# Top-k attention and a routed MLP on one core: GpSimd's difference for the first fold waits for VectorE's minimum of the second fold

## The chip, the core and the metric

The kernel runs on one core of a Trainium2 chip. The engines named here are TensorE (PE in the profile, its weight loads PEld), VectorE (DVE), ScalarE (ACT), GpSimd (POOL) and SyncE (SP), which issues most transfers. Each engine works through its own queue of instructions in order; semaphores make one wait for another. The metric is device time in microseconds (us), from the first instruction to the end of the program. An instruction's row in the profile carries the line of the kernel that issued it (L351 is line 351).

## The reference

The input is attention over 8 batches with 8 heads, 576 tokens and a head size of 64, in which each query keeps only its 32 largest scores, and then a routed MLP with 8 experts: each of the 4608 tokens goes through the one expert with the largest gate.

```python
scores = scale * np.matmul(q, k.transpose(0, 1, 3, 2))
kth = np.partition(scores, -top_k, axis=-1)[..., -top_k:-top_k + 1]
scores = np.where(scores >= kth, scores, -1000000000.0)
attn = np.exp(scores - scores.max(-1, keepdims=True))
attn = attn / (attn.sum(-1, keepdims=True) + 1e-09)
x = (attn @ v).transpose(0, 2, 1, 3).reshape(4608, 512)
...
expert_idx = np.argmax(x @ w_gate, axis=1)
gate_w = softmax(x @ w_gate)[np.arange(4608), expert_idx]
for e in range(8):
    h = np.maximum(x[expert_idx == e] @ w1[e], 0.0)
    y[expert_idx == e] = h @ w2[e]
return gate_w[:, None] * y
```

## The kernel before

**Units and slots.** Two heads of one batch form a unit; there are 32 units. One slot handles two tiles of 128 queries each, with 576 scores for every query. Two units together have 9 slots (8 with two full tiles, one with the tails of 64 queries), so there are 144 slots. They follow each other in `loop()`, in an order that is written out by hand for TensorE, ScalarE and VectorE; GpSimd's instructions keep the order of the program where `in_turn` is put around them. Once the first batch has its tokens sorted into rows of `x_rows`, pieces of the routed MLP are put between the attention's matmuls.

**What a slot does for its scores.** TensorE multiplies queries by keys into PSUM (`products`, L314), three to four slots ahead. ScalarE copies the scores to SBUF (`scores`, L321, the tile `s`), in slot i for slot i + 3. VectorE then folds them (`folds`, `fold`, `fold_on`) and searches the 32nd largest score of each query (`search`). In the first 27 slots ScalarE computes the weights without a mask (`unmasked`, L497), marks the scores under the threshold (`shortfalls`, L470, which waits for the threshold `low`), and TensorE subtracts the marks while it transposes the weights (L516, L517). In the other slots GpSimd takes part in the mask (`less`, L489).

**The folds.** A row of 576 scores is folded in half: `h` holds the 288 larger ones of each pair, `l` the smaller ones. Then `h` is folded again into `few` (144 larger ones) and `hl` (144 smaller ones). `search` looks for maxima in `few` with MAX8 (L415), strikes the found ones out with MATCH_REPLACE8 (L434), and repeats this for four rounds of eight. After the first round the function `lists` adds the eight largest of `l` and twice of `hl` to `few` (L390).

**Which engine makes `l`.** In the first 27 slots the smaller ones aren't all made by VectorE. For most of these slots GpSimd makes `l` in two steps on the scores' bit patterns taken as 32-bit integers: the sum of both halves (`added`, L338), and later the sum minus the larger one (`folds`, L351), which leaves the smaller one. Both steps keep GpSimd's order. Five of the 26 folds of this kind, those whose slot puts the output rows together on GpSimd (`rows`, L655), have their `l` made by VectorE instead (L355). The first slot of all uses `fold`.

**The order around the change.** In slot i, VectorE first makes the folds of slot i + 1 (L346 `h`, L347 `few`, L349 `hl`), then searches slot i, and ends with the threshold `low` (L449). GpSimd's difference for slot i + 1 is put right behind the folds. Behind it in GpSimd's queue come: the sum for slot i + 2 where there is one (L338), which has to wait until `lists` of slot i has read the buffer that it writes (there are two `l` buffers); two small differences (`doubts`, L457 and L460); the bias for the weights (`nbias`, L428); where due, the logits (L641 to L646), the output rows (L655), and indirect transfers of rows (L723). The first MAX8 of the search for slot i + 1, one slot later, waits for that slot's difference, as does `lists`, which reads `l`. There is one buffer for `h`, so that the next `h` waits until the difference has read it.

**Numbers of buffers.** `s` has four buffers, `few` three, `hl` and `l` two, `h` one. SP's queue loads queries, keys and values of the units, the experts' weights and the sorted rows.

Of the kernel before, what the change touches and what calls it, by code (L numbers as in the profile page):

```python
# [13 lines left out]
ALU = mybir.AluOpType  # L14
# [3 lines left out]
WAIT = mybir.DependencyInfo(mybir.DependencyClass.Sync, mybir.DependencyReason.DATA)  # L18
# [27 lines left out]
def kernel(  # L46
# [47 lines left out]
    nc = tc.nc  # L94
# [10 lines left out]
    HF = S // 2  # L105
    QF = S // 4
# [160 lines left out]
    def in_turn(put):  # L267

        if not k.exact:
            tc.keep_in_program_order(put)  # L270
        return put
# [69 lines left out]
    def folds(s, l=None):  # L341

        f = SimpleNamespace(aside=l is not None)
        f.h = k.att.tile([P, 2, HF], F32, name="h", bufs=1)
        f.few = k.att.tile([P, 2, LW], F32, name="few", bufs=3)
        nc.vector.tensor_tensor(f.h, s[:, :, 0, :], s[:, :, 1, :], op=ALU.max)  # L346
        nc.vector.tensor_tensor(f.few[:, :, 0:QF], f.h[:, :, 0:QF], f.h[:, :, QF:HF], op=ALU.max)  # L347
        f.hl = k.att.tile([P, 2, QF], F32, name="hl", bufs=2)
        nc.vector.tensor_tensor(f.hl, f.h[:, :, 0:QF], f.h[:, :, QF:HF], op=ALU.min)  # L349
        if f.aside:  # L350
            f.made = in_turn(nc.gpsimd.tensor_tensor(l, l, f.h[:, :, :].bitcast(I32), op=ALU.subtract)).ins  # L351
            f.l = l[:, :, :].bitcast(F32)
        else:
            f.l = k.att.tile([P, 2, HF], F32, name="l")
            nc.vector.tensor_tensor(f.l, s[:, :, 0, :], s[:, :, 1, :], op=ALU.min)  # L355
        return f
# [791 lines left out]
    with fast:  # L1148
# [224 lines left out]
        def loop():  # L1373
# [16 lines left out]
            for i, (b, g) in enumerate(work):  # L1390
# [11 lines left out]
                if i + 1 < len(work):  # L1402
                    if quick(i):
                        def behind():
                            f_of[i + 1] = folds(s_of[i + 1], l_of.pop(i + 1, None))
                    else:
                        def behind():
                            f_of[i + 1] = fold(s_of[i + 1])

                        then = lambda: fold_on(f_of[i + 1], soon and not k.heavy)  # L1410
                    if i:
                        behind()
                        behind = lambda: None
# [227 lines left out]
```

## Time and profile before

| what | us |
|---|---|
| median of 3 runs | 1280.93 (1280.36 to 1282.18) |
| the profiled execution, its own time | 1280.47 |
| its span, first to last instruction | 1278.9 |
| TensorE busy in the span | 1197.5 (94%) |
| VectorE busy | 1058.1 (83%) |
| ScalarE busy | 922.3 (72%) |
| GpSimd busy | 721.3 (56%) |

The shares are means over stages of different kinds: the folds that the change concerns start between 18.2 and 208.1 us, the attention's slots go on until about 1070 us, and behind that only the routed MLP is left. So the profile is read by stages below, with the table of stretches, the waits between engines, the timeline of single slots, and the rows grouped by line. The mean granted TensorE clock of the execution was 0.97 of full speed.

### The profile page before, as it was taken

Reading aid. Unit: us, or ns where it says so; the run is one execution under the profiler, and the core shown is the slowest. Engines: PE = TensorE matmul, PEld = TensorE weight load, DVE = VectorE, ACT = ScalarE, POOL = GpSimd, SP = SyncE. Lnnn points to the kernel's source line nnn. Section 1 sums busy time; section 2 is a strip of 40 time slices with the busy share of each in tenths; the row PEclk is TensorE's granted clock in tenths of the full one; section 3 lists DMA queues with packets and bytes.
Section 4 is the critical chain, followed back from the end, with each engine's and each line's share of the span. In section 5 each row is a group of like instructions: output and inputs, shape, how many; then the busy total and the mean of one; then the engine's idle time right before and its main releaser. Section 6 shows DMA issues by size and latency. Waiting matters only on the chain. (4 is left out here: it accounts for less than half of the span.)

```text
span 1278.9 us, 26013 instructions
## 1 busy us (share of the span) xinstructions
PE 1197.5 (94%) x8312; PEld 852.9 (67%) x8312; DVE 1058.1 (83%) x4635; ACT 922.3 (72%) x2063; POOL 721.3 (56%) x1006
## 2 busy tenths in 40 slices
PE   6877778799899999999999999999999999999998
PEld 3555555566556665766667667676666667799985
DVE  8999999999999999999999999999999985000000
ACT  4677767898889888988888889888888892111211
POOL 4554454777787786657666775667656762100010
PEclk9788888899999999999999999999999999999999
DMA  5010011653174318542865464456554646995662
GB/s 154 27 34 23 12 31 56 239 189 103 61 268 166 114 55 308 204 137 95 284 229 191 162 234 179 179 187 215 186 195 167 231 162 221 360 352 210 237 238 83
DMA packets 97043, 216.58 MB, mean 169 GB/s; under 512 B 5245, under 2 KB 26237, under 8 KB 96896
## 3 DMA queue, kind: packets, MB, share of 16 engines
q1 hardware_dynamic: 89728, 194.54, 43.6%
q0 software_dynamic: 6352, 19.97, 4.3%
q8 instruction: 67, 1.10, 0.3%
q14 instruction: 80, 0.66, 0.2%
q10 hardware_dynamic: 816, 0.31, 0.1%
HBM read 191.42 MB, written 23.91 MB: 168 GB/s over the span
## 5 line engine op out<-in xcount | busy, mean ns | idle before, releaser
L489 POOL TENSOR_TENSOR w<-s,w 128x576 f32<-128x576 f32 x234 | 331.8, 1439 | 233.8 <-ACT w L480 233.7
L1102 PE MATMUL ph<-xTs,w 128*128 128x128 f32 x1984 | 249.6, 278 | 2.8 <-ACT xTs L993 2.8
L1102 PEld LDWEIGHTS ph<-xTs,w 128*128 128x128 f32 x1984 | 233.7, 192 | 26.8 <-issue 23.1
L1119 PE MATMUL py<-w,hT 128*128 128x512 f32 x496 | 239.0, 603 | 0.5
L415 DVE MAX8 tops<-few 128x8 f32<-128x144 f32 (+3 forms) x864 | 222.5, 292 | 0.0
L314 PE MATMUL sc<-qkb 64*128 64x288 f32 (+1 forms) x1280 | 204.8, 461 | 15.5 <-ACT s L321 11.3
L506 ACT ACTIVATE w<-w,nbias 128x576 f32<-128x576 f32 x234 | 181.2, 785 | 0.9 <-POOL w L489 0.3
L321 ACT COPY s<-sc 128x576 f32<-128x576 f32 x288 | 168.1, 635 | 8.3 <-PE sc L314 8.2
L480 ACT ACTIVATE w<-s,low 128x576 f32<-128x576 f32 x234 | 168.7, 768 | 3.8
L314 PEld LDWEIGHTS sc<-qkb 64*128 64x128 f32 (+1 forms) x1280 | 111.0, 190 | 83.8 <-issue 39.8
L434 DVE MATCH_REPLACE8 few<-tops,few 128x144 f32<-128x144 f32 (+2 forms) x576 | 158.1, 279 | 0.0
L521 ACT COPY wT<-wTm 128x512 f32<-128x512 f32 x234 | 127.2, 594 | 41.2 <-PE wTm L514 40.1
L514 PE MATMUL wTm<-turn,w 128*128 128x128 f32 x936 | 127.7, 277 | 21.6 <-ACT oT L591 11.0
L514 PEld LDWEIGHTS wTm<-turn,w 128*128 128x128 f32 x936 | 108.0, 143 | 56.6 <-issue 22.4
L586 PE MATMUL po<-wT,vb 128*64 128x288 f32 x1024 | 139.5, 415 | 0.0
L1119 PEld LDWEIGHTS py<-w,hT 128*128 128x128 f32 x496 | 84.2, 190 | 74.5 <-issue 72.5
L390 DVE MAX8 few<-l 128x8 f32<-128x288 f32 x288 | 127.0, 441 | 0.0
L1011 POOL DMA_INDIRECT out_dram<-y,xg x36 | 38.4, 1066 | 150.0 <-ACT y L1078 85.4
L586 PEld LDWEIGHTS po<-wT,vb 128*64 128x64 f32 x1024 | 68.3, 138 | 64.8 <-issue 12.5
L390 DVE MAX8 few<-hl 128x8 f32<-128x72 f32 x576 | 99.4, 211 | 0.0
L330 DVE TENSOR_TENSOR h<-s 128x576 f32<-128x576 f32 (+1 forms) x119 | 90.1, 757 | 2.8 <-ACT s L321 2.8
L434 DVE MATCH_REPLACE8 scr<-tops,few 128x168 f32<-128x168 f32 x288 | 88.5, 311 | 0.0
(234 smaller groups left out, 1969.5 us busy)
## 6 DMA issues: line engine op xcount, KB each, us to landing
w<-in_moe_w_dram SPq DMA_DIRECT2D x72, 2048.0 KB, 9.0
qkb<-in_qk_dram SPq DMA_DIRECT2D x31, 608.0 KB, 4.0
vb<-in_v_dram SPq DMA_DIRECT2D x32, 320.0 KB, 3.2
xg<-x_rows SPq DMA_DIRECT2D x36, 257.0 KB, 9.1
x_rows<-blank SPq DMA_DIRECT2D x13, 257.0 KB, 7.4
x_rows<-blank POOLq DMA_DIRECT2D x4, 257.0 KB, 9.3
x_rows<-x,posi POOLq DMA_INDIRECT x40, 3.4
out_dram<-y,xg POOLq DMA_INDIRECT x36, 4.0
```

What stands on the lines that cost most here:

```text
L314: nc.tensor.matmul(ps[rows, j, 0:HF], n.q[d, cols], n.k[d, keys], start=True, stop=True)
L321: lambda m=m, ps=ps: nc.scalar.copy(s[:, m, :, :], ps[:, :, 0:HF]) for m, ps in enumerate(got)
L390: nc.vector.max(out=f.few[:, m, QF + 8 * j:QF + 8 * j + 8], in_=away)
L415: scan = nc.vector.max(out=tops[:, m, r * 8:(r + 1) * 8], in_=src[m]).ins
L434: nc.vector.match_replace(out=src[m] if inside else scr[:, m, :], in_to_replace=tops[:, m, r * 8:(r + 1) * 8], in_values=src[m], imm_value ...
L480: nc.scalar.activation(w[:, m, :], s[:, m, :, :].rearrange("p j k -> p (j k)"), AF.Relu, scale=-STEEP, bias=low[:, m:m + 1],)
L489: k.last_pool = in_turn(nc.gpsimd.tensor_tensor(w[:, m, :], s[:, m, :, :].rearrange("p j k -> p (j k)"), w[:, m, :], op=ALU.subtract)).ins
L506: nc.scalar.activation(w[:, m, :], w[:, m, :], AF.Exp, scale=scale, bias=nbias[:, m:m + 1], accum_out=n.z[:, c:c + 1])
L514: nc.tensor.transpose(to, part(w), ident)
L586: nc.tensor.matmul(po[r, 0:HF], n.v[:, c, r], rhs, start=(c == 0), stop=(c == KC - 1))
L1102: nc.tensor.matmul(ph[:, f, :], n.w1[:, 0, dt, fc * P:(fc + 1) * P], n.xT[:, dt, :], start=(dt == 0), stop=(dt == DT - 1),)
L1119: nc.tensor.matmul(py, hT[:, f, :], n.w2[:, 0, f, :], start=(f == 0), stop=(f == FT - 1))
```

## The change

The difference on GpSimd (L351) is given a further dependency: it must wait until VectorE has finished the minimum of the second fold, `hl`. Before, it waited for `h`, which it reads, and for its own earlier sum. No instruction is added or taken away, and the order of each engine's instructions in the program is the same. The other branch, in which VectorE makes `l`, is as it was.

```diff
         f.hl = k.att.tile([P, 2, QF], F32, name="hl", bufs=2)
-        nc.vector.tensor_tensor(f.hl, f.h[:, :, 0:QF], f.h[:, :, QF:HF], op=ALU.min)
+        last = nc.vector.tensor_tensor(f.hl, f.h[:, :, 0:QF], f.h[:, :, QF:HF], op=ALU.min).ins
         if f.aside:
             f.made = in_turn(nc.gpsimd.tensor_tensor(l, l, f.h[:, :, :].bitcast(I32), op=ALU.subtract)).ins
+            tc.add_manual_dep(f.made, last.name, WAIT)
             f.l = l[:, :, :].bitcast(F32)
```

`WAIT` is a dependency that is kept with a semaphore between the two engines.

## The prediction before the run

> **What bounds the kernel now.** The change touches only the first 27 slots, so I began with the table of stretches: what each engine does in the stage of these slots and behind it (us, then the busy time of TensorE, its weight loads, VectorE, ScalarE and GpSimd, the granted clock, the DMA share).
>
> ```profile
> core 0: us, PE busy (x) PEld busy (x) DVE busy (x) ACT busy (x) POOL busy (x), PEclk, DMA share, GB/s
> 18.24:208.10 189.86, 151.51 (x1330) 100.39 (x1330) 185.79 (x775) 133.51 (x261) 97.07 (x161) 0.85 0.11 32
> 208.10:300.00 91.90, 80.95 (x623) 55.32 (x622) 91.14 (x410) 81.13 (x187) 65.43 (x91) 0.94 0.49 172
> 300.00:900.00 600.00, 580.92 (x3930) 398.51 (x3928) 599.75 (x2636) 524.83 (x1217) 422.53 (x559) 0.99 0.51 180
> 900.00:1070.00 170.00, 169.27 (x1145) 117.95 (x1143) 153.16 (x663) 141.43 (x332) 106.39 (x144) 1.00 0.52 180
> ```
>
> The first row runs from the first to the last fold of the changed kind. VectorE is busy 185.79 of 189.86 us there; the rest is hand-overs between its own instructions. TensorE is idle for 38.35 us. So VectorE sets the pace of this stage, though TensorE has the largest share of the whole span. Next I asked the waits who waits for whom: VectorE's only wait for another engine worth naming is the first row below, and it has no place in the 27 slots' own folds; the other rows (engine, line, what it waited for; total us, times, longest) say that ScalarE and TensorE are the ones that wait.
>
> ```profile
> DVE h L330 <- ACT s L321: 2.8, 3, 2.0
> ACT hT L470 <- DVE low L449: 45.4, 21, 3.5
> PE wTm L516 <- ACT oT L591: 14.6, 9, 2.8
> PE wTm L516 <- ACT xl L616: 13.5, 4, 3.4
> PE sc L314 <- ACT s L321: 9.3, 6, 2.6
> ```
>
> ScalarE stands 45.4 us in 21 waits for the threshold that closes VectorE's search, and TensorE stands behind ScalarE. Then I read one slot in the timeline (start, duration, engine, line):
>
> ```profile
> 25.62 0.76 DVE L346 TENSOR_TENSOR h<-s 128x576 f32<-128x576 f32 x1
> ...
> 26.49 0.46 DVE L347 TENSOR_TENSOR few<-h 128x288 f32<-128x288 f32 x1
> 26.53 1.67 POOL L351 TENSOR_TENSOR l<-l,h 128x576 int32<-128x576 int32 x1 [2.08 <-DVE h L346]
> 26.86 1.66 DVE L349 TENSOR_TENSOR hl<-h 128x288 f32<-128x288 f32 x1
> ...
> 28.45 0.25 DVE L415 MAX8 tops<-few 128x8 f32<-128x96 f32 x1
> ...
> 33.09 0.76 DVE L346 TENSOR_TENSOR h<-s 128x576 f32<-128x576 f32 x1
> ```
>
> The slot takes 33.09 − 25.62 = 7.47 us. GpSimd's difference (L351) starts 0.15 us after h is done. VectorE's two half-width operations behind h have the same shape, yet few takes 0.46 us and hl 1.66 us: hl is under way for as long as GpSimd's difference, and ends at 28.52, 0.32 us after it (26.53 + 1.67 = 28.20). What hl takes without that neighbour stands in the one slot in which GpSimd came late (202.65), held up by transfers that it issues (L723), and in slots where no difference is made at all:
>
> ```profile
> 71.68 0.45 DVE L349 TENSOR_TENSOR hl<-h 128x288 f32<-128x288 f32 x1
> ...
> 202.65 0.45 DVE L349 TENSOR_TENSOR hl<-h 128x288 f32<-128x288 f32 x1
> ...
> 203.80 0.45 DVE L390 MAX8 few<-l 128x8 f32<-128x288 f32 x1
> 204.16 0.35 DVE L390 MAX8 few<-hl 128x8 f32<-128x72 f32 x2
> 204.43 0.44 DVE L390 MAX8 few<-l 128x8 f32<-128x288 f32 x1
> ...
> 202.92 1.03 POOL L723 DMA_INDIRECT x_rows<-x,posi  x1 [0.31 <-issue]
> 203.96 1.44 POOL L351 TENSOR_TENSOR l<-l,h 128x576 int32<-128x576 int32 x1
> ```
>
> So 0.45 us alone, 1.66 us beside the difference: 1.21 us of VectorE's time lost in a slot, on the engine that sets the pace.
>
> **The change, step by step.** It adds no instruction and no transfer. It moves one wait: L351 waits for the end of hl instead of the end of h. The wait on h falls away, since VectorE finishes h before hl. The grouped rows of these slots (busy us in all, mean ns) and those of the single lines (ns, least, median, most) give the sum:
>
> ```profile
> L349 DVE TENSOR_TENSOR hl<-h 128x288 f32<-128x288 f32 x26 | 35.9, 1380 | 0.0
> ...
> L351 POOL TENSOR_TENSOR l<-l,h x21: 1440/1672/1681, 19.1 to 204.0; 128x576 int32<-128x576 int32 x21
> ...
> L338 POOL TENSOR_TENSOR l<-s x20: 1400/1410/1423, 22.2 to 198.3; 128x576 int32<-128x576 int32 x20
> L434 DVE MATCH_REPLACE8 few<-tops,few x98: 233/244/272, 22.6 to 203.6; 128x96 f32<-128x96 f32 x50, 128x120 f32<-128x120 f32 x48
> L390 DVE MAX8 few<-hl x100: 208/211/220, 21.3 to 204.9; 128x8 f32<-128x72 f32 x100
> L390 DVE MAX8 few<-l x50: 434/443/453, 21.0 to 204.4; 128x8 f32<-128x288 f32 x50
> ```
>
> Of 26 folds, 21 have the difference on GpSimd; one of these (202.65 us) came free already. All 26 hl at 0.45 us would be 11.7 us; they took 35.9. **VectorE gets back 35.9 − 11.7 = 24.2 us**, which is 20 × 1.21.
>
> What the difference will lie beside instead: VectorE goes straight on to the search of the slot before (MAX8, MATCH_REPLACE8, the lists at L390). GpSimd's sum L338, the same kind of operation, runs beside such instructions in every slot that has one, and their durations show no second group: L390 stays between 208 and 220 and between 434 and 453 ns over all calls. The lists at 203.80 to 204.43 ran right beside a difference, at 0.45, 0.35 and 0.44 us. I therefore cost the new neighbourhood at nothing on VectorE, and the difference itself at 1.44 us, as there. [...]
>
> The added delay on GpSimd: hl will end at 26.86 + 0.45 = 27.31, so the difference runs from about 27.46 (the same 0.15 us after its releaser) to 28.90, where it ended at 28.20. VectorE's search starts about 27.24 instead of 28.45. Measured from there, the difference ends 1.66 us into the search; before, 0.25 us ahead of it. Who is late for that? In GpSimd's queue behind it stand, by slot, the next sum (L338) or the two doubt differences and nbias:
>
> ```profile
> 30.44 1.41 POOL L338 TENSOR_TENSOR l<-s 128x576 int32<-128x576 int32 x1 [2.23 <-DVE few L390]
> ...
> 81.22 0.45 DVE L390 MAX8 few<-l 128x8 f32<-128x288 f32 x1
> ...
> 82.44 1.41 POOL L338 TENSOR_TENSOR l<-s 128x576 int32<-128x576 int32 x1 [1.46 <-DVE few L390]
> ...
> 167.56 0.56 POOL L428 TENSOR_SCALAR nbias<-tops 128x1 f32<-128x1 f32 x2 [2.10 <-DVE tops L415]
> ```
>
> L338 starts 30.44 − 28.45 = 1.99 us into the search, released by the lists: 0.33 us of cover are left. Behind a slot with the rows, the search begins with the lists (81.22), L338 starts 1.22 us into it (82.44) and would be about 0.4 us late against VectorE. Nothing of this reaches VectorE: the sum is for the fold after next, and this slot's own difference is read a slot later. Without L338 the doubts follow at once and nbias has 2.10 us of idle time ahead. The next h must wait until the difference has read the one h buffer, which it has 3 us earlier (28.90 against 33.09 − 1.21). GpSimd's own transfers into x_rows are the same and stand ahead of the difference (202.92), not behind it. SP's queue issues nothing for this.
>
> What is late next when VectorE is 1.21 us faster: ScalarE. Its rows for the step that waits on the threshold (in brackets the wait ahead of it):
>
> ```profile
> 78.38 1.43 ACT L470 ACTIVATE hT<-s,low 128x576 bf16<-128x576 f32 x2
> 85.99 1.44 ACT L470 ACTIVATE hT<-s,low 128x576 bf16<-128x576 f32 x2 [2.62 <-DVE low L449]
> ...
> 154.99 1.44 ACT L470 ACTIVATE hT<-s,low 128x576 bf16<-128x576 f32 x2 [3.18 <-DVE low L449]
> ...
> 193.58 1.44 ACT L470 ACTIVATE hT<-s,low 128x576 bf16<-128x576 f32 x2 [0.94 <-DVE low L449]
> ```
>
> Of the 20 slots that shorten, 19 end in a wait of 1.4 us or more, and one in 0.94 us (193.58). If every slot had to pay from its own wait, 19 × 1.21 + 0.94 = 23.9 us would remain; and slots lend each other time, because scores are copied to SBUF two slots ahead of their fold. Slots without a wait (78.38) are those behind the rows, whose folds do not shorten, and ScalarE has caught up one slot later. TensorE's 151.51 us of work must fit into 189.86 − 24.2 = 165.7 us, which is 91% even at the low granted clock of 0.85. Behind the stage VectorE goes on at 99 to 100% until 900 us, so what the stage ends earlier passes on one to one: all later transfers hang on places in the slots, not on a time.
>
> **Sum.** The profiled execution took 1280.47 us (span 1278.9): 1280.47 − 24.2 = 1256.3. Against the median of 1280.93, 0.46 above it, this is 1256.7. I forecast **1256.5 us**.
>
> **Rivals.** (a) *ScalarE and TensorE take over part of it.* For the whole gain, TensorE's idle time must fall from 38.35 to about 14 us. If it kept half of it, because the waits on oT and xl come from the order of ScalarE's steps and not from VectorE, the stage would be 151.51 + 19.2 = 170.7 us: a gain of 19.2, 1261.3 us. For it: TensorE has slots without any pause, as this stretch of one slot shows, and the clock in the stage is at 0.85.
>
> ```profile
> 107.81:116.46 8.65, 8.65 (x96) 5.55 (x93) 8.16 (x31) 5.93 (x12) 5.96 (x9) 0.88 0.00 1
> ```
>
> Against it: ScalarE waits for VectorE in every slot that shortens. Chance 0.12.
> (b) *More than the sum.* A second collision sits behind the rows, where few waits for GpSimd's multiply:
>
> ```profile
> 77.62 1.77 POOL L655 TENSOR_TENSOR x<-xl,rz 128x640 f32<-128x640 f32 x1
> ...
> L347 DVE TENSOR_TENSOR few<-h 128x288 f32<-128x288 f32 x26 | 15.7, 605 | 3.3 <-DVE h L346 0.9
> ```
>
> At 0.46 each, 26 few would take 12.0 us, not 15.7. If the moved queue also freed these, 3.7 us more: 1252.6 us. But that multiply hangs on the lists and on nbias of its own slot, as before. Chance 0.03.
> (c) *The change doesn't do what it says:* the difference starts late anyway or something else stretches hl. Then 1280.5 us. Against it: hl is at 0.45 wherever the difference isn't beside it. Chance 0.03.
> (d) *Slower: the difference blocks the search instead of hl.* If MAX8 or MATCH_REPLACE8 stood still while it runs, VectorE would lose up to 1.44 us per slot and get back 1.21: 20 × 0.23 = 4.6 us more, 1285.1 us. It decides once more than 1.21 of the 1.44 us fall on the search. The steady L390 durations speak against it. Chance 0.02.
>
> **From this to the numbers.** The forecast has 0.80. Its own spread is small, from 1254.5 to 1259, for what slots lend each other and for phases of GpSimd and VectorE in later stages. The range takes in (b) below and most of (a) above, up to a gain of 16.5 us: 1252.5 to 1264; (c), (d) and a harder form of (a) are left out. Forecast, (a) and (b) are faster by over 0.2% (2.6 us, about what a measurement of this kernel can tell from no change): 0.95. Within 0.2%: 0.03, from (c). Slower: 0.02, from (d).
>
> **What would show it.** Right: hl at 0.45 in all 26 folds (11.7 us in all), L351 at about 1.42 us and starting behind hl, slots of 6.26 us where they were 7.47, MAX8 and MATCH_REPLACE8 as before, ScalarE's wait for low about 24 us shorter in total, the last changed fold at about 184 us instead of 208. Rival (a) shows as VectorE waiting for ScalarE's copies L321; (d) as MAX8 of over 1 us; (c) as hl at 1.66 still. Wrong would be a stage that ends 24 us earlier with a span that doesn't: then a transfer or TensorE holds the later stages.

## The result and the profile after

The changed kernel takes **1258.47 us** (1258.15 to 1259.00, 4 runs) against 1281.36 us before (1280.36 to 1282.18, 4 runs). The ratio is 0.982, with a 95% interval of 0.9805 to 0.9839. The forecast was 1256.5 us, with a range of 1252.5 to 1264 us.

Two rows of the table of stretches of the changed kernel; the first is cut at the first and the last fold of the changed kind, as before:

```profile
core 0: us, PE busy (x) PEld busy (x) DVE busy (x) ACT busy (x) POOL busy (x), PEclk, DMA share, GB/s
18.37:184.09 165.72, 138.03 (x1317) 92.14 (x1318) 161.66 (x776) 132.64 (x259) 91.25 (x161) 0.93 0.12 37
300.00:900.00 600.00, 584.18 (x3935) 401.19 (x3936) 599.75 (x2622) 523.91 (x1212) 417.57 (x548) 0.99 0.52 182
```

The stage took 189.86 us before and takes 165.72 now: **24.14 us less**, and VectorE's busy time in it fell by 185.79 − 161.66 = 24.13 us. VectorE is still the busy one (161.66 of 165.72), and from 300 to 900 us it is busy for 599.75 of 600 us, as before. One slot in the timeline of the changed kernel shows how:

```profile
30.81 0.76 DVE L346 TENSOR_TENSOR h<-s 128x576 f32<-128x576 f32 x1
31.68 0.46 DVE L347 TENSOR_TENSOR few<-h 128x288 f32<-128x288 f32 x1
32.05 0.45 DVE L349 TENSOR_TENSOR hl<-h 128x288 f32<-128x288 f32 x1
...
32.42 0.41 DVE L416 MAX8 tops<-few 128x8 f32<-128x96 f32 x2
32.65 1.40 POOL L351 TENSOR_TENSOR l<-l,h 128x576 int32<-128x576 int32 x1 [2.23 <-DVE hl L349]
...
37.08 0.76 DVE L346 TENSOR_TENSOR h<-s 128x576 f32<-128x576 f32 x1
```

hl takes 0.45 us, GpSimd's difference starts 0.15 us after its end and lies beside the search, and the slot is 37.08 − 30.81 = 6.27 us long (7.47 before). (From L352 on, lines are one higher than before.) The groups and single lines of the stage:

```profile
L349 DVE TENSOR_TENSOR hl<-h 128x288 f32<-128x288 f32 x26 | 11.7, 450 | 0.0
...
L351 POOL TENSOR_TENSOR l<-l,h x21: 1403/1407/1435, 20.1 to 179.9; 128x576 int32<-128x576 int32 x21
...
L391 DVE MAX8 few<-hl x100: 208/217/223, 20.3 to 180.9; 128x8 f32<-128x72 f32 x100
L391 DVE MAX8 few<-l x50: 434/446/453, 19.9 to 180.4; 128x8 f32<-128x288 f32 x50
```

All 26 hl together take 11.7 us (35.9 before), the difference has 1.41 us in the median (1.67), and the lists of the search keep their 0.22 and 0.45 us with the difference beside them. ScalarE's wait for low and TensorE's waits for oT and xl have become shorter; TensorE's wait for ScalarE's copies of the scores has grown from 9.3 to 11.0 us (total us, times, longest):

```profile
ACT hT L471 <- DVE low L450: 24.3, 20, 3.0
PE sc L314 <- ACT s L321: 11.0, 8, 2.6
...
PE wTm L517 <- ACT xl L617: 8.0, 4, 2.2
PE wTm L517 <- ACT oT L592: 7.4, 7, 2.4
```

**Where the difference went afterwards.** I set the starts of h side by side, fold by fold. From the first changed fold to the last, each of 20 slots is 1.19 to 1.22 us shorter and the others are as long as before, to 0.01 us. From there to the last fold of all (1037.40 and 1015.91 us), 24.01 us shrink to 21.49, in four places: 0.58 us in the slot that begins with the last changed fold (slot 28 in the count of the expectations below), 1.21 at fold 63, 0.32 in all at folds 71 to 73, and 0.46 at fold 77. Two of them in rows. In slot 28 VectorE's reciprocal waits for ScalarE in the changed kernel:

```profile
189.87 0.22 DVE L623 RECIPROCAL rz<-rz 128x10 f32<-128x10 f32 x1 [0.49 <-ACT rz L621]
```

At fold 63 the same kind of collision as in the first stage appears, this time with the mask's difference on GpSimd (L489, now L490). First the kernel before, then the changed one (the rows of both engines in the same slot):

```profile
462.11 3.44 POOL L489 TENSOR_TENSOR w<-s,w 128x576 f32<-128x576 f32 x2 [1.16 <-ACT w L480]
...
463.46 0.43 DVE L361 TENSOR_TENSOR few<-h 128x288 f32<-128x288 f32 x1
463.81 0.44 DVE L369 TENSOR_TENSOR hl<-h 128x288 f32<-128x288 f32 x1
```

```profile
438.71 3.03 POOL L490 TENSOR_TENSOR w<-s,w 128x576 f32<-128x576 f32 x2 [1.17 <-ACT w L481]
...
440.05 0.43 DVE L362 TENSOR_TENSOR few<-h 128x288 f32<-128x288 f32 x1
440.40 1.66 DVE L370 TENSOR_TENSOR hl<-h 128x288 f32<-128x288 f32 x1
```

Both engines have the same instructions at nearly the same distance: GpSimd's pair begins 463.46 − 462.11 = 1.35 us ahead of few in the one and 440.05 − 438.71 = 1.34 us ahead in the other. Yet in the one GpSimd is held up (3.44 us for two) and VectorE isn't, and in the other hl pays 1.66 us. Whether this belongs to the change is the question of the sixth and seventh run.

### The profile page after: what moved, and what is told of

Read it like the earlier page. It is cut to its first block, busy times and chain, and to the rows that moved or that the text cites. A ratio compares the mean times of both kernels' runs of the same rounds, so it can differ in the third digit from the quotient of the medians.

```text
span 1257.4 us, 26013 instructions
## 1 busy us (share of the span) xinstructions
PE 1185.5 (94%) x8312; PEld 845.8 (67%) x8312; DVE 1036.0 (82%) x4635; ACT 922.8 (73%) x2063; POOL 715.3 (57%) x1006
## 5 line engine op out<-in xcount | busy, mean ns | idle before, releaser
L490 POOL TENSOR_TENSOR w<-s,w 128x576 f32<-128x576 f32 x234 | 331.3, 1436 | 235.9 <-ACT w L481 235.9
L314 PE MATMUL sc<-qkb 64*128 64x288 f32 (+1 forms) x1280 | 199.7, 452 | 17.9 <-ACT s L321 13.5
L314 PEld LDWEIGHTS sc<-qkb 64*128 64x128 f32 (+1 forms) x1280 | 107.8, 187 | 85.9 <-issue 39.0
L391 DVE MAX8 few<-l 128x8 f32<-128x288 f32 x288 | 127.2, 442 | 0.0
L391 DVE MAX8 few<-hl 128x8 f32<-128x72 f32 x576 | 99.6, 211 | 0.0
```

The source lines that it names most:

```text
L314: nc.tensor.matmul(ps[rows, j, 0:HF], n.q[d, cols], n.k[d, keys], start=True, stop=True)
L391: nc.vector.max(out=f.few[:, m, QF + 8 * j:QF + 8 * j + 8], in_=away)
L490: k.last_pool = in_turn(nc.gpsimd.tensor_tensor(w[:, m, :], s[:, m, :, :].rearrange("p j k -> p (j k)"), w[:, m, :], op=ALU.subtract)).ins
```

## The experiments

**1. Wait for few instead of hl.** Does any overlap cost VectorE time, or only one in which GpSimd began first?

```diff
-        nc.vector.tensor_tensor(f.few[:, :, 0:QF], f.h[:, :, 0:QF], f.h[:, :, QF:HF], op=ALU.max)
+        last = nc.vector.tensor_tensor(f.few[:, :, 0:QF], f.h[:, :, 0:QF], f.h[:, :, QF:HF], op=ALU.max).ins
...
-        last = nc.vector.tensor_tensor(f.hl, f.h[:, :, 0:QF], f.h[:, :, QF:HF], op=ALU.min).ins
+        nc.vector.tensor_tensor(f.hl, f.h[:, :, 0:QF], f.h[:, :, QF:HF], op=ALU.min)
```

> GpSimd's difference waits for few (L347), one VectorE operation earlier than in the changed kernel. Theory A (the two operations exclude each other, and the one that begins first goes first): hl begins about 0.2 us before the difference is released, so hl stays at 0.45 us and the difference is held up instead (1.6 us or so instead of 1.41); all 20 collisions stay gone, and the time is that of the changed kernel, 1258.5 us within 2.5. Theory B (any overlap with the difference slows VectorE, whichever was first): the difference lies beside most of hl, hl takes 1.3 to 1.7 us in 20 slots, and the time goes back to 1277 to 1281 us.

Measured: 1259.19 us (1258.74 to 1259.41), ratio to before 0.982 (0.9807 to 0.984). A slot of its timeline, and the group of the difference:

```profile
31.18 0.46 DVE L347 TENSOR_TENSOR few<-h 128x288 f32<-128x288 f32 x1
31.55 0.45 DVE L349 TENSOR_TENSOR hl<-h 128x288 f32<-128x288 f32 x1
31.72 1.55 POOL L351 TENSOR_TENSOR l<-l,h 128x576 int32<-128x576 int32 x1 [1.79 <-DVE few L347]
```

The difference now begins 0.17 us after hl and lies beside 0.28 us of it, and hl still takes 0.45 us: GpSimd pays, 1.55 instead of 1.41 us. So in these folds it is not the overlap that costs VectorE time but who begins first. Theory A holds, theory B falls. That the two operations exclude each other altogether, as theory A has it, these rows show only roughly: the difference ends 33.27 − 32.00 = 1.27 us after hl, 0.14 us sooner than its 1.41 us alone would need.

**2. The new wait in every other difference.** Does each slot bring its own 1.21 us?

```diff
-            tc.add_manual_dep(f.made, last.name, WAIT)
+            k.nth = 1 - getattr(k, "nth", 0)
+            if k.nth:
+                tc.add_manual_dep(f.made, last.name, WAIT)
```

> The new wait stands in every other one of the 21 differences; of the 20 that collided before, 10 keep their old wait. Theory A (1.21 us a collision, each slot on its own): hl at 0.45 in 16 folds and at 1.66 in 10, the last fold starts 12.1 us later than in the changed kernel (196.2 instead of 184.1), the time is 1270 us. Rival C (a fixed limit of ScalarE or TensorE takes over at some point, so that the first collisions removed are worth more than the last): clearly under 1270, 1262 to 1266. What the later slots give back (2.6 us with the whole change) should not be half of that under the theory that it comes from races of GpSimd and VectorE in single later slots: 0 to 4 us, in steps of 0.4 to 1.2.

Measured: 1270.37 us (1270.04 to 1270.61), ratio 0.991 (0.9894 to 0.9927). The group of hl:

```profile
L349 DVE TENSOR_TENSOR hl<-h 128x288 f32<-128x288 f32 x26 | 23.8, 916 | 0.0
```

23.8 us lie midway between 11.7 and 35.9. From the first to the last of these folds the stage is 12.08 us longer than in the changed kernel, ten steps of 1.20 to 1.22. Half the dose gives half the gain, and no other engine takes over up to the full dose: rival C falls.

**3. VectorE alone.** What was GpSimd's help worth before?

```diff
-                    if quick(i + 1) and not rows_at(i + 1):
+                    if False:
                         l_of[i + 2] = added(s_of[i + 2])
```

> All l of the first 27 slots are made by VectorE (L356); GpSimd makes neither sum nor difference. Theory A: VectorE pays 0.74 us more in 21 slots than in the changed kernel (a slot in which it makes l took 7.00 us there, one with the difference aside 6.26), but has no collision: 1258.5 + 15.5 = 1274 us, so that it is faster than the kernel before, whose collision cost 1.21 us where the operation taken off VectorE was worth 0.74. Rival (the gain comes from GpSimd's lateness to other work, or from its queue, not from hl): not faster than before, 1281 us or more.

Measured: 1270.07 us (1268.65 to 1270.69), ratio 0.9904 (0.9888 to 0.9921). The folds of one slot and the next h:

```profile
24.89 0.78 DVE L346 TENSOR_TENSOR h<-s 128x576 f32<-128x576 f32 x1
25.77 0.46 DVE L347 TENSOR_TENSOR few<-h 128x288 f32<-128x288 f32 x1
26.15 0.45 DVE L349 TENSOR_TENSOR hl<-h 128x288 f32<-128x288 f32 x1
26.52 0.75 DVE L356 TENSOR_TENSOR l<-s 128x576 f32<-128x576 f32 x1
31.84 0.78 DVE L346 TENSOR_TENSOR h<-s 128x576 f32<-128x576 f32 x1
```

With VectorE doing the whole work, a slot takes 31.84 − 24.89 = 6.95 us: 0.69 more than in the changed kernel and 0.52 less than before. So in the kernel before, an operation that took 0.7 us off VectorE cost it 1.21 us. The rival (the gain comes from GpSimd's lateness to other work) falls. Forecast 1274, measured 4 us less: 0.69 instead of 0.74 us a slot, and with GpSimd's sum and difference gone, few no longer met the multiply of the rows either (all 26 few at 0.46 us), which I hadn't counted. The multiply met another operation of VectorE instead, the threshold `low`:

```profile
101.30 1.26 POOL L656 TENSOR_TENSOR x<-xl,rz 128x640 f32<-128x640 f32 x1
...
101.77 0.81 DVE L450 TENSOR_SCALAR low<-tops 128x2 f32<-128x2 f32 x1
```

low takes 0.14 to 0.17 us elsewhere. In the five slots with a multiply it takes 0.47 to 0.82 us and ends 0.02 or 0.03 us after the multiply (here 102.58 and 102.56), although it reads only one tensor. One low of the changed kernel shows the same: it takes 0.47 us at 191.62 and ends 0.03 us after the multiply (190.80 + 1.26 = 192.06). So low, with its one input, was held up as well. MAX8, which also reads one tensor, and MATCH_REPLACE8 show no such case: over the whole traces of both kernels the 288-wide MAX8 takes 429 to 457 ns and MATCH_REPLACE8 on 96 to 168 columns 233 to 324.

**4. The rows' multiply behind the folds.** The other collision of the stage, between few and GpSimd's multiply for the output rows, stands in the changed kernel as before:

```profile
69.31 1.77 POOL L656 TENSOR_TENSOR x<-xl,rz 128x640 f32<-128x640 f32 x1
...
70.07 1.33 DVE L347 TENSOR_TENSOR few<-h 128x288 f32<-128x288 f32 x1
```

This version gives it the same cure: for the first four units it is issued behind the next slot's folds and waits for their hl.

```diff
+        if behind_folds:
+            tc.add_manual_dep(behind_folds.pop()(), last.name, WAIT)
         if f.aside:
...
             logits(n, lg)
-            rows(n, x)
+            if b * U + u < 2 * EARLY - 2:
+                behind_folds.append(lambda: rows(n, x))
+            else:
+                rows(n, x)
```

> On top of the changed kernel, the multiply for the output rows (L655 before) of the first four units is put behind the folds of the next slot, with a wait for their hl. Theory A: four few at 0.46 instead of 1.2 to 1.6, 3.9 us less collision, and 0.1 to 0.3 us less around it in each of the four slots: the last fold starts 4 to 5 us earlier than in the changed kernel, about 179.5 us, and the time is 1254.2 us (1253 to 1256.5, by what later slots do). Rival: in these four slots GpSimd's queue is the longest already, and the multiply ahead of sum, doubts and nbias makes nbias and so ScalarE's weights late by 1.3 us each: no gain, 1258.5 us or more.

Measured: 1255.22 us (1252.70 to 1256.18), ratio 0.9786 (0.9769 to 0.9802). The slot of the rows, and the group of few:

```profile
69.75 0.46 DVE L347 TENSOR_TENSOR few<-h 128x288 f32<-128x288 f32 x1
70.16 0.46 DVE L349 TENSOR_TENSOR hl<-h 128x288 f32<-128x288 f32 x1
70.70 1.26 POOL L659 TENSOR_TENSOR x<-xl,rz 128x640 f32<-128x640 f32 x1 [1.66 <-DVE hl L349]
...
L347 DVE TENSOR_TENSOR few<-h 128x288 f32<-128x288 f32 x26 | 11.9, 458 | 3.3 <-DVE h L346 0.9
```

few loses its 3.8 us (15.7 to 11.9), and the stage is 3.25 us shorter than in the changed kernel, a little less than the 4 to 5 us I had added up.

**5. A write in the difference's place.** In the kernel before, the difference is replaced by a fill of `l` that waits for h and reads nothing; the smaller ones of the first fold are left out of the search.

```diff
-            f.made = in_turn(nc.gpsimd.tensor_tensor(l, l, f.h[:, :, :].bitcast(I32), op=ALU.subtract)).ins
+            f.made = in_turn(nc.gpsimd.memset(l, 0)).ins
+            tc.add_manual_dep(f.made, big.name, WAIT)
```

> The kernel before, with GpSimd's difference replaced by a fill of l with zeros that still waits for h alone: it writes the same tile at the same place and reads nothing; the smaller ones of the first fold are left out of the search. Theory A1 (what collides is the second input of VectorE's operation with GpSimd's reads): hl at 0.45 us in all folds though the fill lies beside few or hl. Rival A2 (any GpSimd operation that touches SBUF holds VectorE's operations with two inputs): hl, or few, longer by what is left of the fill when they begin, so over 0.6 us in 20 folds if the fill takes over 0.8 us.

Measured: 1256.11 us in one run. A slot and the single line of hl:

```profile
24.95 0.46 DVE L347 TENSOR_TENSOR few<-h 128x288 f32<-128x288 f32 x1
24.97 0.58 POOL L351 MEMSET l<- 128x576 int32 x1 [2.01 <-DVE h L346]
25.33 0.45 DVE L349 TENSOR_TENSOR hl<-h 128x288 f32<-128x288 f32 x1
...
L349 DVE TENSOR_TENSOR hl<-h x26: 444/451/454, 19.1 to 184.4; 128x288 f32<-128x288 f32 x26
```

The fill is shorter than I had assumed (0.58 us), so the test is a weaker one: hl begins when 0.22 us of the fill are left, and would have taken some 0.1 to 0.2 us more under A2 (0.1 if 0.13 us of hl can lie beside its opponent's end, as in the kernel before, where hl ended 0.32 us after the difference). It took 0.444 to 0.454 us in all 26 folds. So this write doesn't hold hl up. That the difference's reads do is my inference from what is left, as far as a fill can stand for the writes of a difference; that the second input of hl is the other party was the assumption of A1. Neither is shown: no run here has tried a fold with one input.

**6 and 7. Both kernels once more,** to see what of the later losses belongs to the change.

> The changed kernel once more, to see what belongs to one execution in the later slots. If the 2.6 us given back there come from races of GpSimd and VectorE that an execution decides anew, the long hl of fold 63 and the short stretches at folds 71 to 73 fall elsewhere or are gone, while the wait for ScalarE's rz in slot 28 (0.49 us) stays. If they follow from the shifted order of work, all of them stand where they stood, within 0.1 us. The 20 hl of the first stage are at 0.45 us either way.

> The kernel before once more. The 20 hl at 1.66 us stand as they were, and no wait for rz in slot 28. If single executions decide the later races, some of the later stretches move (fold 63 long, or fold 45 short, or folds 73 and 77 other than 0.83 and 0.59 us); if they belong to the kernel, the list is the same.

Measured: 1258.49 us for the changed kernel, 1283.56 for the kernel before. From the starts of the folds (first of the changed kind, last of it, last of all), for these two executions, the two of the comparison above, and that of run 8:

| execution | first to last changed fold, us | from there to the last fold of all, us |
|---|---|---|
| before | 189.86 | 829.30 |
| before, again (7) | 189.85 | 832.91 |
| changed | 165.72 | 831.82 |
| changed, again (6) | 165.71 | 831.75 |
| changed, third (8) | 165.73 | 829.77 |

The first column repeats to 0.02 us; the second doesn't. The kernel before, unchanged, needed 3.6 us more in its second execution, and had the long hl at fold 63 that its first one hadn't:

```profile
463.19 3.04 POOL L489 TENSOR_TENSOR w<-s,w 128x576 f32<-128x576 f32 x2 [1.17 <-ACT w L480]
...
464.52 0.43 DVE L361 TENSOR_TENSOR few<-h 128x288 f32<-128x288 f32 x1
464.88 1.67 DVE L369 TENSOR_TENSOR hl<-h 128x288 f32<-128x288 f32 x1
```

In turn, the changed kernel had no long hl there in its second and third execution. The wait for rz in slot 28, which I had expected to stay, is gone in the second execution of the changed kernel and 0.55 us in the third; in the second of the kernel before, where I had expected none, it is 0.28 us. So the 2.5 us between the first two traces (829.30 and 831.82) need no cost of the change: the later slots differ from one execution to the next by 3.6 us in the kernel before and by 2.1 us in the changed one. In the kernel before, 2.6 of the 3.6 us are folds that took longer (h, l, few and hl behind the stage took 285.5 us in all, and 288.1 in the second execution); what makes up the 2.1 us was not worked out.

**8 and 9. The changed kernel and version 4 side by side,** five rounds on one chip.

> The changed kernel, timed beside the next one: 1258.5 us (1257.5 to 1259.5), 23 to 24 us under the kernel before on the same chip, if the stage's 24.1 us are all of the change and single executions of both kernels scatter by 1 to 3 us in later slots.

> The version with the rows' multiply behind the folds, timed beside the changed kernel on the same chip: theory A expects it 3.3 to 4 us faster than that, 1254.6 us (1253.5 to 1255.8). The rival (nbias late, the gain given back in the same slots) expects less than 1 us.

Measured: 1258.12 us (1255.58 to 1258.53), ratio 0.9802 (0.9787 to 0.9816), and 1254.86 us (1252.69 to 1258.09), ratio 0.9776 (0.9763 to 0.979), beside 1283.03 us before (1279.67 to 1283.59, 9 runs). The changed kernel is 24.9 us under the kernel before, where I had expected 23 to 24. Version 4's median is 3.3 us lower, as it was in its first timing (1255.22 against 1258.47). It is the best of the versions by the medians, but single runs of the two overlap, since the later slots scatter by as much as it gains: in version 4's second trace they took 833.73 us, beside 829.77 in the changed kernel's.

## Why the prediction was right, step by step

- *Who sets the pace, and what hl costs.* Right. The stage is shorter by the time that VectorE is less busy, 24.14 us beside 24.13. The sum forecast 24.2 from 35.9 − 11.7; measured are 20 slots of 1.19 to 1.22 us. Experiment 2 shows that they add up one by one, experiment 1 that it is the order of the two operations that matters.
- *Nothing is lost in the search.* Right: L391's durations are as they were, 208 to 223 and 434 to 453 ns. The medians, 217 and 446 ns, are a few ns above those before, but experiment 3, with no difference at all, has 217 and 448. MATCH_REPLACE8 shows no second group either (233 to 273 ns). The slower rival (d) falls.
- *The delay on GpSimd hurts no one.* Right: behind the difference the sum L338 still waits 0.36 or 0.37 us in 11 slots, where 0.33 us of cover were worked out. In five others, four of them behind the rows, where it was to come late, it has no wait left (73.20 us is one), and none of these slots lost anything of its gain.
- *ScalarE and TensorE keep up.* Right in the stage, but the working for TensorE was not. ScalarE's waits for low went from 45.4 to 24.3 us (21.1 less, not 24), and TensorE's three waits from 37.4 to 26.4. The prediction took TensorE's 151.51 us of busy time as fixed, so that its idle time had to fall to about 14 us. It fell from 38.35 to 165.72 − 138.03 = 27.69 us only, since the busy time fell too. Nor was the slot without a pause a limit: it took 8.65 us before and takes 7.44 now, and TensorE is busy throughout in both. What there was of rival (a) is the wait for rz in slot 28, 0 to 0.55 us in three executions of the changed kernel and 0 to 0.28 in two of the kernel before. In the traces of runs 1 and 9, whose stage is as short or shorter, it is 1.13 and 1.29 us, in those of runs 2 to 5 there is none; whether the change makes it more frequent stays open.
- *(b)* Right in its place: those 3.7 us stayed where they were (few takes 15.7 us in both), and experiment 4 gets them by the means that the change used.
- *One to one to the end.* Right for the mean, too sure for a single pair of executions. I took one execution as the base, and 1280.47 us was a good one: over the further runs the kernel before has medians of 1281.4 to 1283.0. The gain by medians is 22.9 us in the first comparison and 24.9 in the last, around the 24.2 forecast; the time came out 2.0 us above the forecast, of which the low base is 0.4 to 2.1 us, by which of these medians one takes; the rest is no more than the later slots scatter. No term of the sum failed. The 1254.5 to 1259 us that I gave for the forecast's own spread held it.

## What to carry to other kernels

An operation moved to GpSimd wasn't free for VectorE here: the 20 hl that began 0.18 to 0.33 us behind GpSimd's difference took 1.65 to 1.67 us instead of 0.45 and ended 0.31 to 0.32 us after it, and the help cost more than it saved (1.21 us against 0.7). Look in the timeline for two operations of the same shape with different durations, and let GpSimd's operation wait until VectorE goes on with operations whose durations stay the same beside it: here MAX8 (0.22 and 0.45 us in the lists) and MATCH_REPLACE8 (0.23 to 0.32 us in the stage, by its columns), but not the TENSOR_SCALAR of experiment 3 (0.47 to 0.82 us instead of 0.14 to 0.17). When a trace shows small losses far behind a change, run the unchanged kernel again before explaining them.

## What the runs showed of the hardware that I had not expected

TensorE's busy time in the stage fell from 151.51 to 138.03 us for the same work, at a granted clock of 0.93 of full speed instead of 0.85; the products of the two, 128.8 and 128.4 us, are nearly equal. That shortened nothing here, as VectorE set the pace, but it made the rival in which TensorE takes over weaker than its 91% had suggested. Not all of it is the change's: the second execution of the kernel before had 146.76 us at 0.89 in a stage of the same length, while all three of the changed kernel had 0.93 (over the whole executions 0.970 and 0.973 before, 0.982 to 0.985 changed). What set the clock was not tested.

The distance that the profile records doesn't say which engine goes first when the two are this close. At fold 63 hl was long with GpSimd's pair 1.34 us ahead of few (changed kernel) and 1.33 us ahead (run 7), and short with 1.35 us (kernel before) but also with 1.33 us (438.57 − 437.24 in run 5). Each time 1.2 us of VectorE's time hung on it.
